# Hand-ordered steps of an attention kernel: subtractions moved from VectorE to GpSimd, one weight operation per step, mask limits called later

## The chip, the cores and the metric

The kernel runs on one core of a Trainium2 chip. The metric is the time of one execution on the device, in microseconds (us). Before the change three runs took 440.40, 440.41 and 440.67 us (median 440.41). The core has five engines that run beside each other: PE (TensorE, matmuls), DVE (VectorE), ACT (ScalarE), POOL (GpSimd) and SP (SyncE, which issues transfers here). PEld is PE's loading of weights.

## The reference

Four batches of 768 tokens with 8 heads of 64 go through an attention with a mask (8 global keys, and the last 96 tokens) and a bias by distance; what comes out goes through a feed-forward stage with a convolution over three tokens and a gate. Everything is in float32, the weights of the second stage come as float64.

```
scores = q @ k.T / sqrt(64) - slope[head] * dist;  scores = where(keep, scores, -1e9)
a = softmax(scores);  x = (a @ v), heads side by side            # 4 x 768 x 512
h = relu(x @ w_in)                                               # 4 x 768 x 1024
conv = cw[0] * h[t-1] + cw[1] * h[t] + cw[2] * h[t+1]
out = (h * sigmoid(conv)) @ w_out                                # 4 x 768 x 512
```

## The kernel before

Attention goes in 32 jobs (a batch, a half `u` of the tokens, a pair of heads) of three blocks of 128 rows. A block is a *step*; there are 96 of them, numbered `s`. In a step PE makes the scores of two heads (L381), DVE adds the bias from a table and takes the row's limit (L408), ACT takes the exponential and its sum (L425), PE transposes the result (L450, L452), ACT copies it out of PSUM (L455), and PE multiplies by v (L501). Because PE's single-pass float32 format (fp32r) is not exact enough by itself, every operand of the feed-forward stage is kept as a high part (rounded to fp32r) and a low part (what the rounding left), and a product is three matmuls: high by high, high by low, low by high.

Steps 0 to 13 (`HAND = 14`) are written out by hand in `by_hand`: there each engine takes its instructions in the order of the code. From step 14 on a scheduler orders the instructions by a model of its own; it may put an instruction that has no one to wait for into an earlier gap. In the first four jobs of the hand-ordered steps the softmax is divided late: PE spreads the inverse sums over a PSUM tile (`spread`, L476), ACT copies it (`factors`, L484), DVE multiplies (`scaled`, L488), ACT rounds the mixed heads to their high part (`mixed_high`, L513) and DVE subtracts to get the low part (`mixed_low`, L517, tile `xl`). In steps 6, 9 and 12 PE takes one slice of the first feed-forward product of a job that is done (`mm1_early`, L560): `wih` by `xh`, `wih` by `xl`, `wil` by `xh`. Some small matmuls on a constant tile (`warm`, L168) stand in every step.

Beside that the weights are turned from float64 words into high and low parts, in 16 pieces of 128x512. For a piece ACT makes a first value from the low words (L305, `weight_tail`), DVE puts in the bits of the high words with two operations (L311, L313), POOL rounds to the high part (L318, `weight_high`), and DVE subtracts for the low part (L324, `weight_low`). `work("dve", 0.1)` takes one operation from a list of these; by hand it is called twice in an even step and once in an odd one. `limits` (L239 to L242) are four tiny DVE operations that test whether the mask's two numbers are in range; only the very end of the program reads what they leave.

Of the kernel before, what the change touches and what calls it, by code (L numbers as in the profile page):

```python
# [9 lines left out]
F32 = mybir.dt.float32  # L10
# [5 lines left out]
ALU = mybir.AluOpType  # L16
# [9 lines left out]
NB = TB // P  # L26
# [14 lines left out]
HAND = 14  # L41
# [26 lines left out]
def fast_path(tc, io):  # L68
    nc = tc.nc
    V, A, G, T = nc.vector, nc.scalar, nc.gpsimd, nc.tensor  # L70
# [95 lines left out]
    def warm(n):  # L166
        for _ in range(n):
            T.matmul(wp[:, TB:], wz, wz, start=True, stop=True)  # L168
# [69 lines left out]
    def limits():  # L238
        V.tensor_scalar(odd[:, 0:1], nl, 1.0, None, ALU.is_lt)  # L239
        V.tensor_scalar(odd[:, 1:2], nl, float(NPREV + 1), None, ALU.is_gt)  # L240
        V.tensor_scalar(odd[:, 2:3], ng, float(NGLOB), None, ALU.is_gt)
        V.tensor_reduce(bad, odd, axis=mybir.AxisListType.X, op=ALU.max)  # L242
        G.memset(ones, 1.0)
# [36 lines left out]
    def weight_planes(i):  # L280
        if i < NK:
            h, l = wih[:, i], wil[:, i]
        else:
            j = i - NK
            h = woh[:, 2 * j : 2 * j + 2].rearrange("p f d -> p (f d)")
            l = wol[:, 2 * j : 2 * j + 2].rearrange("p f d -> p (f d)")
        return (x.rearrange("p (f n) -> p f n", f=NF) for x in (h, l))
# [27 lines left out]
    def weight_high(i, half):  # L315
        t = wt[i, half]
        h, l = weight_planes(i)
        G.tensor_copy(h[:, half * HF : (half + 1) * HF], t)  # L318

    def weight_low(i, half):  # L320
        t = wt[i, half]
        h, l = weight_planes(i)
        sl = slice(half * HF, (half + 1) * HF)
        V.tensor_tensor(l[:, sl], t, h[:, sl].bitcast(F32), ALU.subtract)  # L324

    words, top, TOP = [], {}, 0x38000000

# [33 lines left out]
    st_s, st_pt, pv, xt, sums = {}, {}, {}, {}, {}  # L361
# [4 lines left out]
    def free(s):  # L366
        return s < NB * FREE

    def scores(s):
        m, i = steps[s]  # L370
        b, u, hp = jobs[m]
        w = NKC[u]
        first = u == 0 and i == 0
        n = W0 if first else WIN
        k0 = key_start(u, i)
        both = ps_s.tile([P, 2, 256], F32, tag="s", name=f"s{s}")
        sp = [both[:, 0], both[:, 1]]
        for j in range(2):
            if m < NATIVE:
                rq, rk = raw[m]  # L380
                last_mm[s] = T.matmul(  # L381
                    sp[j][:, :n],
                    rq[:, j, i * P : (i + 1) * P],
                    rk[:, k0 : k0 + n],
                    start=True,
                    stop=True,
                )
                continue
            qh, ql, kk = qk[m]
            for n_, (q_, st, sp_) in enumerate(((qh, True, False), (ql, False, True))):  # L390
                last_mm[s] = T.matmul(  # L391
                    sp[j][:, :n],
                    q_[:, j * TB + i * P : j * TB + (i + 1) * P],
                    kk[:, j * w + k0 : j * w + k0 + n],
                    start=st,
                    stop=sp_,
                )
        st_s[s] = (sp, n, first)
# [73 lines left out]
    def spread(m):  # L472
        for i in range(NB):
            for j in range(2):
                k = 2 * (NB + i) + j
                T.matmul(  # L476
                    wp[64 * j : 64 * j + 64, i * P : (i + 1) * P],
                    sums[m][:, k : k + 1].to_broadcast([P, D]),
                    ident, start=True, stop=True,
                )  # L480
# [31 lines left out]
        xt[m] = (xh, xl)  # L512
        A.activation(xh, pv[m], AF.Copy)  # L513

    def mixed_low(m):
        xh, xl = xt[m]
        cur["mixed"] = V.tensor_tensor(xl, pv[m], xh.bitcast(F32), ALU.subtract)  # L517

    def mixed(m):
        mixed_high(m)  # L520
        mixed_low(m)

    def ends(s):
        return s >= 0 and s % NB == NB - 1
# [189 lines left out]
    queue, cur = [], {}  # L714
# [25 lines left out]
    chores = {"dve": [], "pool": []}  # L740

    def work(eng, budget):
        q = chores[eng]
        while q and budget > 0 and q[0][0] <= cur["s"]:
            _, cost, fn, args = q.pop(0)
            fn(*args)
            budget -= cost
# [15 lines left out]

    def piece_high(i, half):
        weight_high(i, half)
        chores["dve"].insert(2, (0, 0.6, piece_low, (i, half)))

    def piece_low(i, half):
        weight_low(i, half)
        done[i, half] = cur["s"]  # L770

    def need(*pieces):
# [19 lines left out]
    def by_hand(s):  # L792
        m, i = steps[s]
        p, q = s - 1, s - 2
        scores(s)
        if q >= 0 and free(q):
            block(*steps[q])
        if ends(q):
            spread(q // NB)
        mm1_early(s)  # L800
        warm(WARM[s + 1])
        if ends(q):
            factors(q // NB)
        if p >= 0 and free(p):
            transposes(p)
        maxima(s)
        exps(s)
        if ends(s - 3):
            mixed_low((s - 3) // NB)
        if ends(p):  # L810
            inverses(p // NB)
        if ends(q):
            scaled(q // NB)
            mixed_high(q // NB)
        if p >= 0 and not free(p):
            normalise(p)
        if i == 0 and m + 1 < NPAIR:
            table(2 * m + 2, X=G)
            table(2 * m + 3, X=G)
        for _ in range(2 - s % 2 if s else 1):  # L820
            work("dve", 0.1)
        if s == HAND - 1:
            mixed_low(q // NB)
        if s == 5:
            limits()
        if s in (4, 6):
            conv_weights((s - 4) // 2)
        work("pool", 1.3)

    hand = True  # L830
    for s in range(len(steps) + LAG_V + 1):
        cur["s"] = s
        m, i = steps[s] if s < len(steps) else (len(jobs), -1)
        if s < HAND:
            by_hand(s)
        else:
            if hand:
                hand = False
                cur["auto"] = True
                manual.__exit__(None, None, None)  # L840
                queue.extend(ffn(0))
            if s < len(steps):
                scores(s)
                maxima(s)
                exps(s)
            e = s - LAG_V - 1
            if e >= SPU and e % SPU == SPU - 1:
                queue.extend(ffn(e // SPU))
            left = SPU - (e + 1) % SPU + 1
            if e + 1 >= len(steps) - SPU:  # L850
                left += 1
            if e < SPU - 1:
                left += SPU
            k = -(-sum(cost for cost, _, _ in queue) // left)
            if ends(e) and not free(e):
                with tc.high_priority():
                    mixed(e // NB)
            if s <= len(steps):
                normalise(s - 1)
            if s < LAG_V + SPU:  # L860
                mm1_early(s)
            k0 = int(k * SHARE[e % 2])
            fill(k0)
            if ends(s - LAG_V) and not free(s - LAG_V):
                values((s - LAG_V) // NB)
            if s < len(steps) + LAG_T and not free(s - LAG_T):
                transposes(s - LAG_T)
            fill(k - k0)
            if s < len(steps):
                budget = DECODE_LATER[min((s - HAND) // 3, len(DECODE_LATER) - 1)]  # L870
                with tc.issue_after(last_ttr[s].ins):
                    work("dve", budget)
                    work("pool", 1.2)
        if s == len(steps):
            for k in range(3):
                check_load()
        if s == HINT:
            with tc.issue_after(last_exp[s].ins):
                tc.mark_branch_hint_location(
                    "general", "LikelyTaken", [mybir.EngineType.Activation]  # L880
                )
        if s == 0:
            for k in range(len(order)):
                chain(*order[k])
            start_piece(0)
            load_v(0)
            start_piece(1)
            load(2)
            start_piece(2)
            load_v(1)  # L890
            start_piece(3)
            load_conv_weights()
        if i < 2:
            prep(m + 1, i)
        if i == 0:
            if 1 <= m < NATIVE - 2:
                load(m + 2)
        elif i == 1 and m + 2 >= NATIVE:
            load(m + 2)
        if m < FREE and s > NB and i == NB - 1:  # L900
            load_v(m + 1)
        elif m > FREE and i == 0:
            load_v(m)
# [203 lines left out]
```

## Time and profile before

| | |
|---|---|
| median of three runs | 440.41 us |
| the profiled execution | 440.63 us, its span in the trace 438.8 us |
| busy: PE / DVE / ACT / POOL | 427.0 / 345.1 / 285.2 / 225.4 us |
| granted clock of PE | 1.0 of full speed throughout |
| steps 0 to 13 in the trace | from about 7 to 43 us |

Busy time is that of the records of an engine. PE's records overlap each other, since matmuls are pipelined, so what one matmul costs is read from the distance between two starts. A record's line (L324) is that of the kernel before; names of tiles stand as written<-read. In the timeline a bracket at a row's end is the engine's idle time before that instruction and what ended it.

### The profile page before, as it was taken

The numbers are of one execution on the slowest core, as the hardware profiler recorded it, in microseconds if no ns is written. First come the engines' busy times: TensorE is split into PE (matmuls) and PEld (weight loads), VectorE is DVE, ScalarE is ACT, GpSimd is POOL, SyncE is SP. The second block draws the span as 40 slices with busy tenths as digits, with TensorE's granted clock in tenths as the row PEclk, the third lists the DMA queues.
The fourth block names the chain that finished last, engine by engine and source line by source line (L and its number), as shares of the span: only waits on it lengthen the run. The fifth ranks groups of instructions, "written<-read, shape, count | busy, mean of one in ns | idle before, by whom it ended". The sixth has DMA issues, their size and how long they took to land.

```text
span 438.8 us, 10010 instructions
## 1 busy us (share of the span) xinstructions
PE 427.0 (97%) x3566; PEld 404.6 (92%) x3566; DVE 345.1 (79%) x894; ACT 285.2 (65%) x771; POOL 225.4 (51%) x324
## 2 busy tenths in 40 slices
PE   9899979999999999999999999999999999999996
PEld 8677967889999999999999999999999999999996
DVE  6797899979999988767989797867999868556500
ACT  2778688597797866647885767647885866136311
POOL 4312789955735963557668843557668631022000
PEclk9999999999999999999999999999999999999999
DMA  8876864322245234353354224442243467800111
GB/s 256 269 229 183 257 176 154 83 83 91 92 122 160 80 111 136 104 176 94 105 150 152 51 101 134 149 141 85 92 162 120 124 242 240 271 26 0 49 50 55
DMA packets 22570, 58.77 MB, mean 134 GB/s; under 512 B 2928, under 2 KB 6256, under 8 KB 22512
## 3 DMA queue, kind: packets, MB, share of 16 engines
q1 hardware_dynamic: 18608, 51.56, 37.7%
q10 hardware_dynamic: 3904, 6.49, 4.1%
q8 instruction: 30, 0.49, 0.5%
q14 instruction: 28, 0.23, 0.2%
HBM read 51.75 MB, written 6.29 MB: 132 GB/s over the span
## 4 chain that ended last, share of the span: by engine, by line
PE 78%; DVE 12%; ACT 6%; issue 2%; POOL 1%; ACTq 0%; DVEq 0%; POOLq 0%
PE o L652 27%; PE h L539 25%; PE pv L501 7%; PE s L391 5%; PE t L450 4%; PE t L452 3%; DVE s L408 3%; PE s L381 3%; ACT pbuf L425 3%; PE warm L168 2%; DVE c L587 2%; DVE c L586 1%; PE o L922 1%; ACT pt L455 1%; DVE w L313 1%
## 5 line engine op out<-in xcount | busy, mean ns | idle before, releaser
L443 POOL TENSOR_SCALAR pbuf<-pbuf,mm 128x232 f32<-128x232 f32 (+1 forms) x156 | 112.3, 732 | 65.1 <-DVE mm L437 41.0
L425 ACT ACTIVATE pbuf<-s,mm 128x232 f32<-128x232 f32 (+1 forms) x192 | 83.0, 440 | 51.8 <-DVE mm L408 38.1
L408 DVE CUSTOM_DVE_ANT_0 s<-s,tab 128x232 f32<-128x232 f32 (+1 forms) x192 | 73.1, 381 | 9.8 <-PE s L391 4.8
L652 PE MATMUL o<-woh,gh 128*128 128x256 f32 x368 | 77.2, 288 | 0.0
L652 PE MATMUL o<-wol,gh 128*128 128x256 f32 x368 | 76.1, 282 | 0.0
L585 POOL TENSOR_SCALAR c<-hbuf,cw 128x382 f32<-128x382 f32 (+1 forms) x64 | 46.1, 723 | 57.8 <-ACT hbuf L549 55.1
L652 PE MATMUL o<-woh,gl 128*128 128x256 f32 x368 | 72.9, 279 | 0.0
L455 ACT ACTIVATE pt<-t 128x512 f32<-128x512 f32 (+1 forms) x96 | 53.7, 566 | 15.0 <-PE t L452 11.5
L539 PE MATMUL h<-xh,wih 128*128 128x384 f32 x252 | 58.2, 348 | 0.3 <-ACT ob L658 0.2
L539 PE MATMUL h<-xl,wih 128*128 128x384 f32 x252 | 58.0, 345 | 0.0
L652 PEld LDWEIGHTS o<-wol,gh 128*128 128x128 f32 x368 | 57.2, 189 | 0.7
L652 PEld LDWEIGHTS o<-woh,gh 128*128 128x128 f32 x368 | 56.6, 189 | 0.7
L539 PE MATMUL h<-xh,wil 128*128 128x384 f32 x252 | 56.7, 344 | 0.0
L652 PEld LDWEIGHTS o<-woh,gl 128*128 128x128 f32 x368 | 56.2, 189 | 0.1
L586 DVE SCALAR_TENSOR_TENSOR c<-hbuf,cw,c 128x382 f32<-128x382 f32 (+1 forms) x64 | 45.2, 712 | 13.4 <-POOL c L585 13.0
L450 PE MATMUL t<-ident,pbuf 128*128 128x128 f32 x192 | 47.6, 276 | 0.9 <-POOL pbuf L443 0.9
L539 PEld LDWEIGHTS h<-xh,wih 128*128 128x128 f32 x252 | 43.4, 189 | 1.4 <-ACT x L484 0.5
L539 PEld LDWEIGHTS h<-xh,wil 128*128 128x128 f32 x252 | 43.8, 188 | 0.6
L549 ACT ACTIVATE hbuf<-h 128x384 f32<-128x384 f32 x64 | 31.2, 492 | 20.2 <-PE h L539 20.1
L587 DVE SCALAR_TENSOR_TENSOR c<-hbuf,cw,c 128x382 f32<-128x382 f32 (+1 forms) x64 | 43.4, 681 | 0.5
L539 PEld LDWEIGHTS h<-xl,wih 128*128 128x128 f32 x252 | 43.3, 189 | 0.3
L501 PE MATMUL pv<-pt,v 128*64 128x128 f32 (+1 forms) x664 | 40.9, 268 | 0.9 <-ACT pt L455 0.9
(123 smaller groups left out, 844.6 us busy)
## 6 DMA issues: line engine op xcount, KB each, us to landing
v<-in_vv SPq DMA_DIRECT2D x32, 384.0 KB, 3.7
wr<-in_w SPq DMA_DIRECT2D x16, 512.0 KB, 4.4
check<-in_w SPq DMA_DIRECT2D x16, 512.0 KB, 4.1
rq<-in_qk SPq DMA_DIRECT2D x20, 384.0 KB, 3.2
rk<-in_qk SPq DMA_DIRECT2D x12, 504.0 KB, 4.0
out<-ob ACTq DMA_DIRECT2D x23, 256.0 KB, 2.5
rk<-in_qk SPq DMA_DIRECT2D x8, 400.0 KB, 3.6
qz<-in_qt SPq DMA_DIRECT2D x22, 96.0 KB, 4.7
```

Of the source, the lines that this page charges most:

```text
L408: last_ttr[s] = V.tensor_tensor_reduce(out=sp[j][:, :n], in0=sp[j][:, :n], in1=tb, scale=-0.125, scalar=3.0e38, op0=ALU.add, op1=ALU.min, ...
L425: last_exp[s] = A.activation(pb[:, j * WIN : j * WIN + n], sp[j][:, :n], AF.Exp, bias=mm[:, j : j + 1], scale=-1.0, accum_out=total[:, j : ...
L443: G.tensor_scalar(x, x, inv, 1.0, ALU.mult, ALU.mult)
L450: T.transpose(pt[:, 0, j], pb[:, j * WIN : j * WIN + P], ident)
L455: last_ev[s] = A.activation(sb[:, :k], pt[:, :k], AF.Copy)
L501: T.matmul(pv[m][64 * j : 64 * j + 64, i * P + q : (i + 1) * P], vt[m][:n, i, c, 64 * j : 64 * j + 64], sb[:n, c, j, q:], start=c == 0, st ...
L539: T.matmul(ps[:, :TB], w_[:, k, fs], x_, start=part == 0 and k == 0, stop=part == 2 and k == NK - 1,)
L549: A.activation(half, ps[:, :TB], AF.Relu, scale=0.5)
L585: G.tensor_scalar(c, *tap(1), 1.0, ALU.mult, ALU.mult)
L586: V.scalar_tensor_tensor(c, *tap(0), c, ALU.mult, ALU.add)
L587: V.scalar_tensor_tensor(c, *tap(2), c, ALU.mult, ALU.add)
L652: T.matmul(ps[:, c], g_[:, f], w_[:, f, c], start=f == part == k == 0, stop=f == NF - 1 and part == 2 and k == 1,)
```

## The change

Low parts of weights whose rounding falls in a hand-ordered step are made by POOL, right behind that rounding, and so are the low parts of the mixed heads of jobs 0 to 2; `work("dve", 0.1)` is called once in each hand-ordered step; `limits` is called after the last step.

```diff
--- before.py
+++ after.py
@@ -317,11 +317,11 @@
         h, l = weight_planes(i)
         G.tensor_copy(h[:, half * HF : (half + 1) * HF], t)
 
-    def weight_low(i, half):
+    def weight_low(i, half, X):
         t = wt[i, half]
         h, l = weight_planes(i)
         sl = slice(half * HF, (half + 1) * HF)
-        V.tensor_tensor(l[:, sl], t, h[:, sl].bitcast(F32), ALU.subtract)
+        X.tensor_tensor(l[:, sl], t, h[:, sl].bitcast(F32), ALU.subtract)
 
     words, top, TOP = [], {}, 0x38000000
 
@@ -512,9 +512,9 @@
         xt[m] = (xh, xl)
         A.activation(xh, pv[m], AF.Copy)
 
-    def mixed_low(m):
+    def mixed_low(m, X=V):
         xh, xl = xt[m]
-        cur["mixed"] = V.tensor_tensor(xl, pv[m], xh.bitcast(F32), ALU.subtract)
+        cur["mixed"] = X.tensor_tensor(xl, pv[m], xh.bitcast(F32), ALU.subtract)
 
     def mixed(m):
         mixed_high(m)
@@ -763,10 +763,13 @@
 
     def piece_high(i, half):
         weight_high(i, half)
-        chores["dve"].insert(2, (0, 0.6, piece_low, (i, half)))
-
-    def piece_low(i, half):
-        weight_low(i, half)
+        if cur["s"] < HAND:
+            piece_low(i, half, G)
+        else:
+            chores["dve"].insert(2, (0, 0.6, piece_low, (i, half, V)))
+
+    def piece_low(i, half, X):
+        weight_low(i, half, X)
         done[i, half] = cur["s"]
 
     def need(*pieces):
@@ -806,7 +809,7 @@
         maxima(s)
         exps(s)
         if ends(s - 3):
-            mixed_low((s - 3) // NB)
+            mixed_low((s - 3) // NB, G)
         if ends(p):
             inverses(p // NB)
         if ends(q):
@@ -817,12 +820,9 @@
         if i == 0 and m + 1 < NPAIR:
             table(2 * m + 2, X=G)
             table(2 * m + 3, X=G)
-        for _ in range(2 - s % 2 if s else 1):
-            work("dve", 0.1)
+        work("dve", 0.1)
         if s == HAND - 1:
             mixed_low(q // NB)
-        if s == 5:
-            limits()
         if s in (4, 6):
             conv_weights((s - 4) // 2)
         work("pool", 1.3)
@@ -872,6 +872,7 @@
                     work("dve", budget)
                     work("pool", 1.2)
         if s == len(steps):
+            limits()
             for k in range(3):
                 check_load()
         if s == HINT:
```

The order in which each engine then has its instructions differs most in these places. Numbers behind a name tell buffers apart and are counted anew in each program. On POOL, from the first rounding of a weight piece (step 2) on, first before, up to step 11:

```order
L318 CAST wih<-w_0_279 128x512
L221 TENSOR_SCALAR tab<-setup 128x360 x2
L318 CAST wih<-w_0_282 128x512
L243 MEMSET misc 128x1
L221 TENSOR_SCALAR tab<-setup 128x360 x2
L318 CAST wih<-w_0_316 128x512
L318 CAST wih<-w_0_397 128x512
L318 CAST wih<-w_1_474 128x512
L318 CAST wih<-w_1_548 128x512
```

and after, up to step 8 (`wil` is the low part of a piece, `xl` that of the mixed heads):

```order
L318 CAST wih<-w_0_279 128x512
L324 TENSOR_TENSOR wil<-w_0_279,wih 128x512
L221 TENSOR_SCALAR tab<-setup 128x360 x2
L318 CAST wih<-w_0_282 128x512
L324 TENSOR_TENSOR wil<-w_0_282,wih 128x512
L517 TENSOR_TENSOR xl_391<-x_377,xh_390 128x384
L221 TENSOR_SCALAR tab<-setup 128x360 x2
L318 CAST wih<-w_0_350 128x512
L324 TENSOR_TENSOR wil<-w_0_350,wih 128x512
L517 TENSOR_TENSOR xl_509<-x_495,xh_508 128x384
L318 CAST wih<-w_0_427 128x512
L324 TENSOR_TENSOR wil<-w_0_427,wih 128x512
```

Each rounding now has a subtraction behind it, and the first `xl` stands behind the second piece's rounding and subtraction. On DVE, the weight operations and the mixed heads of steps 4 and 5 before:

```order
L488 TENSOR_TENSOR x_380<-pv_287,x_380 128x384
L311 SCALAR_TENSOR_TENSOR w_0_316<-wr_0_247,w_0_316 128x512
L324 TENSOR_TENSOR wil<-w_0_279,wih 128x512
L250 TENSOR_SCALAR setup<-setup 128x24
L252 TENSOR_SCALAR cw<-setup 128x24
L253 SCALAR_TENSOR_TENSOR cw<-setup,cw 128x24
L408 ISA s_404,mm_422<-s_404,tab 128x232
```

and after:

```order
L488 TENSOR_TENSOR x_377<-pv_287,x_377 128x384
L313 SCALAR_TENSOR_TENSOR w_0_282<-wr_0_247,w_0_282 128x512
L250 TENSOR_SCALAR setup<-setup 128x24
L252 TENSOR_SCALAR cw<-setup 128x24
L253 SCALAR_TENSOR_TENSOR cw<-setup,cw 128x24
L408 ISA s_402,mm_420<-s_402,tab 128x232
```

What stands in step 4 is now the second bit operation of piece 1, which its rounding on POOL needs; before, that operation stood in step 3. On ACT, the end of step 12 and step 13 before:

```order
L425 ACTIVATE pbuf_215,mm_684<-s_661,mm_684 128x232 x2
L431 ACTIVATE mm_684<-mm_684,misc 128x2
L305 ACTIVATE w_1_693<-wr_1_519 128x512
L305 ACTIVATE w_0_761<-wr_0_625 128x512
L484 ACTIVATE x_719<-warm 128x384
L425 ACTIVATE pbuf_216,mm_721<-s_700,mm_721 128x232 x2
```

and after:

```order
L425 ACTIVATE pbuf_215,mm_676<-s_653,mm_676 128x232 x2
L431 ACTIVATE mm_676<-mm_676,misc 128x2
L484 ACTIVATE x_712<-warm 128x384
L425 ACTIVATE pbuf_216,mm_714<-s_693,mm_714 128x232 x2
L431 ACTIVATE mm_714<-mm_714,misc 128x2
L513 ACTIVATE xh_721<-x_712 128x384
L441 ACTIVATE pbuf_215<-pbuf_215,mm_676 128x232
L305 ACTIVATE w_1_728<-wr_1_540 128x512
L305 ACTIVATE w_0_756<-wr_0_620 128x512
```

Two first values of weight pieces (L305) that stood ahead of the last `factors` now stand behind it. And on DVE, ahead of step 0, where `limits` (L239 to L242) stand after:

```order
L209 SCALAR_TENSOR_TENSOR loc<-setup,num,ge 128x128
L239 TENSOR_SCALAR misc<-num 128x1
L240 TENSOR_SCALAR misc<-num 128x1
L241 TENSOR_SCALAR misc<-num 128x1
L210 SCALAR_TENSOR_TENSOR setup<-setup,num,loc 128x128
L242 TENSOR_REDUCE misc<-misc 128x1
L213 SCALAR_TENSOR_TENSOR loc<-keep,num,loc 128x8
```

Before, these four stood in step 5; the scheduler has put them among the first operations on the mask.

## Rows read from the trace of the kernel before

**Rows 1.** windows of all engines: start:end, length, busy us (instructions), PE clock, DMA.

```profile
20.00:40.00 20.00, 18.95 (x186) 14.94 (x186) 17.99 (x65) 14.55 (x48) 3.25 (x4) 1.00 0.67 198
...
60.00:80.00 20.00, 17.21 (x128) 14.55 (x128) 18.77 (x56) 14.20 (x43) 17.51 (x27) 1.00 0.51 159
...
200.00:300.00 100.00, 100.00 (x851) 97.07 (x850) 83.49 (x220) 68.37 (x184) 63.59 (x82) 1.00 0.38 117
```

**Rows 2.** PE in order of time: start, length, instruction, [idle before <- what ended it].

```profile
21.39 0.62 PE L501 MATMUL spare<-pt,v 128*64 128x128 f32 x8 [0.68 <-ACT pt L455]
...
22.22 0.34 PE L560 MATMUL h<-xl,wih 128*128 128x384 f32 x1
...
29.85 0.33 PE L560 MATMUL h<-xl,wih 128*128 128x384 f32 x1
...
37.70 0.34 PE L560 MATMUL h<-xl,wih 128*128 128x384 f32 x1
...
41.31 1.00 PE L381 MATMUL s<-rk,qz 128*128 128x232 f32 x4
```

**Rows 3.** DVE by line and shape: busy us, mean ns | idle before.

```profile
L324 DVE TENSOR_TENSOR wil<-w,wih 128x512 fp32r<-128x512 f32 x8 | 5.4, 678 | 0.0
...
L517 DVE TENSOR_TENSOR xl<-x,xh 128x384 fp32r<-128x384 f32 x4 | 2.2, 554 | 0.0
```

**Rows 4.** POOL in order of time.

```profile
8.01 0.68 POOL L217 TENSOR_TENSOR setup<-setup,keep 128x232 f32<-128x232 f32 x1
...
9.57 0.10 POOL L235 MEMSET misc<- 128x1 f32 x1
...
24.50 1.00 POOL L318 CAST wih<-w 128x512 fp32r<-128x512 f32 x1 [5.84 <-DVE w L313]
27.83 0.62 POOL L318 CAST wih<-w 128x512 fp32r<-128x512 f32 x1 [2.32 <-DVE w L313]
```

**Rows 5.** DVE in order of time, where it stands beside POOL.

```profile
20.52 0.18 DVE L253 SCALAR_TENSOR_TENSOR cw<-setup,cw 128x24 f32<-128x24 uint32 x1
...
24.96 0.59 DVE L255 SCALAR_TENSOR_TENSOR setup<-setup 128x24 int32<-128x24 int32 x1
```

**Rows 6.** DVE in order of time, steps 4 and 5.

```profile
19.03 0.68 DVE L311 SCALAR_TENSOR_TENSOR w<-wr,w 128x512 int32<-128x512 int32 x1
...
20.62 0.40 DVE L408 CUSTOM_DVE_ANT_0 s<-s,tab 128x232 f32<-128x232 f32 x1
```

**Rows 7.** ACT in order of time, job 1.

```profile
27.60 0.54 ACT L513 ACTIVATE xh<-x 128x384 fp32r<-128x384 f32 x1
```

**Rows 8.** DVE in order of time, steps 10 and 11.

```profile
34.70 0.68 DVE L313 SCALAR_TENSOR_TENSOR w<-wr,w 128x512 int32<-128x512 int32 x1
...
35.90 0.40 DVE L408 CUSTOM_DVE_ANT_0 s<-s,tab 128x232 f32<-128x232 f32 x1
...
36.72 0.55 DVE L517 TENSOR_TENSOR xl<-x,xh 128x384 fp32r<-128x384 f32 x1
```

**Rows 9.** ACT in order of time, steps 12 and 13.

```profile
40.81 1.21 ACT L305 ACTIVATE w<-wr 128x512 f32<-128x512 uint32 x2
41.93 0.47 ACT L484 ACTIVATE x<-warm 128x384 f32<-128x384 f32 x1
```

**Rows 10.** DVE in order of time, ahead of step 0.

```profile
7.22 0.23 DVE L215 TENSOR_SCALAR loc<-keep,num 128x8 f32<-128x8 f32 x1
7.86 0.30 DVE L408 CUSTOM_DVE_ANT_0 s<-s,tab 128x128 f32<-128x128 f32 x1 [0.41 <-PE s L381]
```

**Rows 11.** DVE in order of time, limits in step 5.

```profile
22.51 0.15 DVE L239 TENSOR_SCALAR misc<-num 128x1 f32<-128x1 f32 x1
...
22.88 0.29 DVE L408 CUSTOM_DVE_ANT_0 s<-s,tab 128x128 f32<-128x128 f32 x1
```

**Rows 12.** POOL by line and shape: busy us, mean ns | idle before.

```profile
L443 POOL TENSOR_SCALAR pbuf<-pbuf,mm 128x232 f32<-128x232 f32 x134 | 100.5, 761 | 47.6 <-DVE mm L437 27.4 <-ACT pbuf L425 8.4 <-ACT pt L455 4.3
...
L216 POOL TENSOR_SCALAR keep<-loc 128x232 f32<-128x232 f32 x1 | 0.4, 387 | 5.3 <-DVE loc L215 5.3
```

## The prediction

> **What bounds the kernel now.** I read the windows first. PE stands in nearly every microsecond: 18.95 of 20 us in the window of the hand-ordered steps, all 100 of the window from 200 to 300 us, and only 17.21 from 60 to 80 us [rows 1]. DVE, which the change relieves, is at 17.99 of 20 us in the first of these windows, so it looks like the bottleneck by its share, but its share doesn't say that PE waits for it. That is read from PE's own timeline: in steps 5 to 7 its one long wait is 0.68 us at 21.39, and what ends it is ACT's copy (L455), not DVE [rows 2]. Around it matmuls follow each other without a gap, `warm` ones among them. So the hand-ordered steps are bound by PE, with about 1 us of waiting in 20, and a shorter DVE can give back no more than a part of that. What counts is whether something PE waits for gets later. The three early slices of the feed-forward product are such places: PE takes `xl` at 22.22, 29.85 and 37.70 us [rows 2], in its fixed order, and everything behind it in that order waits too.
>
> **What DVE loses.** In the hand-ordered steps six subtractions for weights at 0.68 us and three for mixed heads at 0.55 us leave DVE [rows 3]: 6 x 0.68 + 3 x 0.55 = 5.7 us of records. The number of bit operations doesn't change (13 calls in place of 19, and the six subtractions are gone), so the same seven pieces are begun and six finished when step 14 comes. I cost this gain at nothing of itself, since PE hides it: PE's next instruction doesn't come earlier when the bias (L408) is done earlier. Transfers of weight words are issued when L313 has read a buffer, so half of them now go one step later; they are used several steps on, and I cost that at nothing too.
>
> **What POOL gets.** Nowhere before does POOL subtract a tile of this size. The nearest row is its addition of two SBUF tiles, 128x232 in 0.68 us (L217); its smallest instruction, a memset, is 0.10 us [rows 4]. Taking 0.10 as fixed: 0.10 + 0.58 x 512/232 = 1.37 us for a weight piece and 0.10 + 0.58 x 384/232 = 1.05 us for mixed heads. I take these, since the row has the same operation with two inputs. The lower end is POOL's rounding, one input, 0.62 us for 512 columns [rows 4], so 0.47 for 384. The upper end is the pace of L443, whose mean is 761 ns where a like operation by itself took 387 ns [rows 12]: a factor of 1.97, thus 2.7 and 2.07 us.
>
> The rounding itself took 0.62 us at 27.83 and 1.00 us at 24.50 [rows 4]. At 24.96 a DVE operation on 24 columns took 0.59 us, where its like took 0.18 us [rows 5]: it ends when POOL's rounding ends. POOL and DVE thus hold each other up where DVE reads two SBUF tiles. The Trainium skill says the same as a rule (SBUF — State Buffer, section "Who interferes with whom"): a DVE instruction with two SBUF inputs and a GpSimd instruction that reads SBUF exclude each other, and the later one blocks until the first is through; these two rows agree. So on POOL a chain of rounding, subtraction, `xl` isn't only slower than on DVE, a DVE bit operation can come in between.
>
> **Step 6.** DVE's bit operation at 19.03 in step 4 is now piece 1's second one (L313) in place of L311 [rows 6]. It starts no earlier, because the multiplication ahead of it hangs on ACT and PE. Two such operations fill 34.70 to 35.90 [rows 8], so one is 0.60 us: done at 19.63. POOL rounds until 20.25 and subtracts until 21.62. DVE's next bias operation comes at 20.02 in place of 20.62 [rows 6], as L324 is gone, takes some 0.97 us, and the bit operation behind it is then blocked from 20.99 to 21.62. If POOL goes on at once, `xl` is done at 21.62 + 1.05 = 22.67; if DVE's 0.60 us come first, at 23.27. PE wanted it at 22.22. It is late by 0.45 to 1.05 us; I take 0.75.
>
> **Step 9.** The high part of job 1 ends at 27.60 + 0.54 = 28.14 [rows 7], POOL has long done its piece, and `xl` would be there at 28.14 + 1.05 = 29.19, ahead of 29.85 [rows 2]. No new wait; both move by the same 0.75.
>
> **Step 12.** L313 for piece 4 starts at 34.70 [rows 8], now 35.45, and ends at 36.05. Rounding to 36.67, subtraction to 38.04, `xl` to 39.09, or 39.69 behind a DVE bit operation. PE wanted it at 37.70: 1.39 to 1.99 late in all, I take 1.7. Before, DVE made this `xl` at 36.72 [rows 8], right behind its bias operation, because there it had no piece ahead of it.
>
> **Step 13.** Here something is won. PE is done with what `factors` (L484) reads when it begins the next scores at 41.31 [rows 2], but ACT is at two first values of weight pieces from 40.81 on and comes to L484 at 41.93 [rows 9]. They now stand behind. That gives 41.93 - 41.31, less a hand-over, 0.5 us; L484 is followed by the exponentials that step 15's scores wait for, so the 0.5 us is on the path.
>
> **The limits.** They aren't at the end: in the order they stand ahead of step 0. Their cost there is what it was in step 5, 22.88 - 22.51 = 0.37 us [rows 11]. Before step 0 DVE has 0.41 us of idle time [rows 10], which hides it on DVE; POOL's part of the table, which waits for L215, gets later by 0.37 and step 1's first bias operation by some 0.1. In step 5 the removal is hidden by PE like the rest.
>
> **The sum.** 1.7 - 0.5 + 0.1 = +1.3 us at step 14. From there on PE's order is nearly that of before and PE is full, so I carry it to the end. Against the profiled execution of 440.63 us (438.8 of span and 1.83 around it) that is 441.93; the median lies 0.22 lower, so 441.7 us.
>
> The Trainium skill (GPSIMD Engine Reference, section "Elementwise — side-by-side cycle accounting") gives 2.6 cycles per element for two inputs because both share one read port, at 1.2 GHz: an estimate of 1.11 and 0.83 us and a fixed part. With 0.1 us fixed, step 6 would be late by 0.5, step 12 by 1.1 in all, and the sum +0.7, 441.1 us. Its table under "Engine selection" says of an elementwise operation on a tile to use VectorE; the row of L217 bears that out.
>
> **The rivals.**
> - *POOL keeps up, faster (0.25).* If the subtraction runs at the pace of the rounding, `xl` is there at 20.25 + 0.62 + 0.47 = 21.34, before PE wants it, and in step 12 too. Then the change has only gains: of the 0.68 us wait for ACT at most all (ACT's L305 no longer stands ahead of that copy), and 0.5 in step 13, less 0.1: -1.1 us, 439.3. For it: POOL is almost idle in these steps, 3.25 of 20 us [rows 1]. Against it: L217. The point from which it decides is where rounding, subtraction and `xl` together take under 2.6 us (22.22 - 19.63); by my values they take 3.04.
> - *The delay is taken up later, no change (0.2).* From 60 to 80 us PE stands still for 2.8 us [rows 1], waiting for others. If the scheduler's other order there has fewer such waits, the 1.3 us vanish: 440.4. Against it: what PE waits for there hangs on steps that begin later too.
> - *The two engines block each other at L443's pace (0.1).* With 2.7 and 2.07 us, step 6 is late by 2.8 to 3.4 and step 12 by 6.1 to 6.7; +5.9, 446.1. Against it: that mean is of later stages, where DVE's convolution and gate operations stand beside POOL.
> - My forecast has 0.45; its own range is 441.2 to 443.2.
>
> **How the numbers follow.** A difference under 0.2% (0.9 us) can't be told from none, thus faster is below 439.5 and slower above 441.3. The forecast lies above it; with the skill's figure it would lie just within. Slower: 0.45 and 0.1, that is 0.55. Same: 0.2. Faster: 0.25. The range reaches from the faster rival, 439.3, to 444.0, where half of the rival with blocking engines is left out.
>
> **What would show it.** Right: POOL's subtractions of 128x512 at 1.2 to 1.5 us; waits of PE of about 1 us for `xl` from POOL in steps 6 and 12, none in step 9; DVE's bit operations of odd steps stretched beyond 0.68 us; L484 of step 13 right behind PE; PE's later timeline moved by 1 to 2 us. Wrong: no wait of PE on L517; subtractions near 0.7 us; or the same step 14, and a difference that arises only between 50 and 140 us.

## The result and the profile after: 2.2 us slower

The changed kernel takes 442.65 us (median of six runs, 442.39 to 444.34), the one before in the same runs 440.49; the ratio is 1.0057, with a 95% interval of [1.0046, 1.0068]. Three slow runs are not counted in this document (469.48 and 1465.27 us of the kernel before, 469.55 us of e3 below). The changed kernel is slower, as forecast, and by more than the 1.3 us forecast. The profiled execution took 443.03 us with a span of 441.1, against 440.63 and 438.8: +2.3 us in the span. The busy time of PE is 427.0 us in both, so PE has no more work; it stands idle more. Where, the windows tell first.

The windows after, in the columns of [rows 1]:

```profile
20.00:40.00 20.00, 16.82 (x164) 12.86 (x162) 16.21 (x51) 13.43 (x44) 12.37 (x13) 1.00 0.63 203
60.00:80.00 20.00, 17.33 (x139) 14.15 (x135) 18.95 (x55) 16.37 (x49) 19.18 (x26) 1.00 0.53 166
200.00:300.00 100.00, 100.00 (x850) 97.10 (x849) 82.75 (x216) 68.40 (x187) 62.97 (x81) 1.00 0.38 118
```

From 20 to 40 us PE was busy 18.95 us and is now 16.82; from 60 to 80 it gains 0.1. The loss is in the hand-ordered steps and nowhere else in these three. Between 12 and 44 us PE's waits of the changed kernel, grouped (us in total, times, longest), have a first line that the kernel before doesn't have:

```profile
PE h L560 <- POOL xl L517: 2.5, 2, 1.3
```

PE of the changed kernel in order of time, at the places of [rows 2]:

```profile
20.82 0.62 PE L501 MATMUL spare<-pt,v 128*64 128x128 f32 x8 [0.30 <-ACT pt L455]
21.37 0.45 PE L560 MATMUL h<-xh,wih 128*128 128x384 f32 x1
23.00 0.44 PE L560 MATMUL h<-xl,wih 128*128 128x384 f32 x1 [1.19 <-POOL xl L517]
...
30.12 0.62 PE L501 MATMUL pv<-pt,v 128*64 128x128 f32 x8 [0.46 <-ACT pt L455]
...
30.95 0.34 PE L560 MATMUL h<-xl,wih 128*128 128x384 f32 x1
...
40.09 0.44 PE L560 MATMUL h<-xl,wih 128*128 128x384 f32 x1 [1.32 <-POOL xl L517]
...
43.80 1.00 PE L381 MATMUL s<-rk,qz 128*128 128x232 f32 x4
...
45.48 0.85 PE L381 MATMUL s<-rk,qz 128*128 128x232 f32 x3
```

And the scores of step 15 in the kernel before:

```profile
43.33 1.05 PE L381 MATMUL s<-rk,qz 128*128 128x232 f32 x4
```

A wait isn't a delay. In step 6 PE stands 1.19 us for `xl`, but the matmul is only 23.00 - 22.22 = 0.78 us later than before, because PE's matmuls ahead of it start 0.57 us earlier (20.82 against 21.39). Of this, 0.38 us is the wait for ACT's copy, which shrank from 0.68 to 0.30 us. The other 0.19 is there before: step 6's scores start at 19.91 against 20.10. That much says little, since over all eleven profiles of this document these scores start between 19.78 and 20.10 us. The delay against before then goes +0.78 (step 6), +1.10 (step 9), +2.39 (step 12), +2.49 (step 14's scores, 43.80 against 41.31) and +2.15 (step 15's scores, 45.48 against 43.33). The last matmul starts at 437.22 against 434.92, +2.30: what is lost by step 15 is carried to the end.

What PE waits for is on POOL. POOL of the changed kernel in order of time, to set beside [rows 4]:

```profile
19.58 0.61 POOL L318 CAST wih<-w 128x512 fp32r<-128x512 f32 x1 [2.07 <-DVE w L313]
20.28 1.27 POOL L324 TENSOR_TENSOR wil<-w,wih 128x512 fp32r<-128x512 f32 x1
21.51 1.44 POOL L517 TENSOR_TENSOR xl<-x,xh 128x384 fp32r<-128x384 f32 x1
...
29.10 1.00 POOL L517 TENSOR_TENSOR xl<-x,xh 128x384 fp32r<-128x384 f32 x1 [2.60 <-ACT xh L513]
...
31.40 1.30 POOL L324 TENSOR_TENSOR wil<-w,wih 128x512 fp32r<-128x512 f32 x1
36.57 0.61 POOL L318 CAST wih<-w 128x512 fp32r<-128x512 f32 x1 [3.87 <-DVE w L313]
37.26 1.82 POOL L324 TENSOR_TENSOR wil<-w,wih 128x512 fp32r<-128x512 f32 x1
39.03 1.00 POOL L517 TENSOR_TENSOR xl<-x,xh 128x384 fp32r<-128x384 f32 x1
```

Two chains stand there without idle time: rounding, subtraction, `xl`. They begin at 19.58 and 36.57 and end when PE's wait ends. In step 9 `xl` finds POOL free. Where no DVE operation holds it up, a subtraction takes 1.27 to 1.30 us and an `xl` 1.00. The 1.44 and the 1.82 stand beside bit operations of DVE, and some of these are stretched too. DVE of the changed kernel in order of time:

```profile
20.97 1.13 DVE L311 SCALAR_TENSOR_TENSOR w<-wr,w 128x512 int32<-128x512 int32 x1
...
31.58 1.67 DVE L311 SCALAR_TENSOR_TENSOR w<-wr,w 128x512 int32<-128x512 int32 x1
...
35.82 0.68 DVE L313 SCALAR_TENSOR_TENSOR w<-wr,w 128x512 int32<-128x512 int32 x1
...
37.24 0.69 DVE L311 SCALAR_TENSOR_TENSOR w<-wr,w 128x512 int32<-128x512 int32 x1
```

The one at 31.58 began when POOL's subtraction of 31.40 to 32.70 was under way, and ends 0.55 us behind it. The one at 37.24 began 0.02 us before POOL's subtraction and took its ordinary 0.69, while POOL's took 1.82 instead of 1.28. In these two pairs, whoever comes first keeps the other out.

ACT of the changed kernel in order of time; the last row is to be set beside the second of [rows 9]:

```profile
28.90 0.68 ACT L305 ACTIVATE w<-wr 128x512 f32<-128x512 uint32 x1
29.46 0.61 ACT L455 ACTIVATE pt<-t 128x512 f32<-128x512 f32 x1
...
44.06 0.49 ACT L484 ACTIVATE x<-warm 128x384 f32<-128x384 f32 x1 [0.67 <-PE warm L168]
```

L484 now follows 44.06 - 43.80 = 0.26 us behind the start of the scores, before 41.93 - 41.31 = 0.62: the gain of step 13 is 0.36 us. The first two rows concern step 9; there L455 stood ahead of L305 in the kernel before:

```profile
28.36 0.60 ACT L455 ACTIVATE pt<-t 128x512 f32<-128x512 f32 x1 [0.23 <-PE t L452]
```

### The profile page after: what moved, and what is told of

Same layout as the page of the kernel before. It is cut to its first block, busy times and chain, and to the rows that moved or that the text cites. A ratio compares the mean times of both kernels' runs of the same rounds, so it can differ in the third digit from the quotient of the medians.

```text
span 441.1 us, 10009 instructions
## 1 busy us (share of the span) xinstructions
PE 427.0 (97%) x3566; PEld 403.6 (91%) x3566; DVE 342.8 (78%) x885; ACT 285.2 (65%) x771; POOL 240.1 (54%) x333
## 4 chain that ended last, share of the span: by engine, by line
PE 78%; DVE 9%; ACT 5%; POOL 5%; issue 2%; DMA 1%; ACTq 0%; DVEq 0%
PE o L652 29%; PE h L539 25%; PE pv L501 7%; PE s L391 6%; PE t L450 4%; PE t L452 3%; ACT pbuf L425 2%; POOL pbuf L443 2%; DVE s L408 2%; DVE c L587 1%; PE s L381 1%; DVE c L586 1%; PE o L923 1%; DMA nn<-in_nn 1%; POOL wil L324 1%
## 5 line engine op out<-in xcount | busy, mean ns | idle before, releaser
L443 POOL TENSOR_SCALAR pbuf<-pbuf,mm 128x232 f32<-128x232 f32 (+1 forms) x156 | 114.4, 744 | 68.7 <-DVE mm L437 50.5
L585 POOL TENSOR_SCALAR c<-hbuf,cw 128x382 f32<-128x382 f32 (+1 forms) x64 | 47.7, 747 | 57.5 <-ACT hbuf L549 54.5
L455 ACT ACTIVATE pt<-t 128x512 f32<-128x512 f32 (+1 forms) x96 | 54.1, 566 | 21.3 <-PE t L452 17.6
L450 PE MATMUL t<-ident,pbuf 128*128 128x128 f32 x192 | 48.4, 277 | 2.8 <-POOL pbuf L443 2.0
L452 PE MATMUL t<-ident,pbuf 128*128 128x128 f32 x160 | 39.9, 276 | 2.5 <-POOL pbuf L443 2.1
```

Of the source, the lines that this page charges most:

```text
L443: G.tensor_scalar(x, x, inv, 1.0, ALU.mult, ALU.mult)
L450: T.transpose(pt[:, 0, j], pb[:, j * WIN : j * WIN + P], ident)
L452: T.transpose(pt[:, 1, j], pb[:, j * WIN + P : j * WIN + 256], ident)
L455: last_ev[s] = A.activation(sb[:, :k], pt[:, :k], AF.Copy)
L585: G.tensor_scalar(c, *tap(1), 1.0, ALU.mult, ALU.mult)
```

## The experiments

The theory: the loss is `xl` on POOL, late because the weight piece's subtraction stands ahead of it there. The rivals: the stretched DVE operations make the loss; the weight pieces on POOL by themselves make it; the place of the limits makes it. Edits are to the changed kernel where nothing else is said, and "ratio" is the time over that of the kernel before.

**Mixed low parts back on DVE (e1).** Weights stay on POOL.

```diff
-            mixed_low((s - 3) // NB, G)
+            mixed_low((s - 3) // NB)
```

> The changed kernel with the low parts of the mixed heads (xl) back on DVE; the low parts of the weights stay on POOL. Theory (PE waits for xl, which stands on POOL behind a rounding and a subtraction): PE's waits of 1.19 and 1.32 us go, 440.0 to 440.8 us. Rival (DVE's bit operations, stretched to 1.1 to 1.7 us by POOL's subtractions, are what delays the steps): they stay stretched, 442 us or more.

Measured: 439.95 us (11 runs, 439.81 to 440.61); against before the ratio is 0.999 [0.9981, 0.9998]. PE's waits for POOL are gone, as the theory has it, and the time lies 0.05 us below its range. The part of the change that is left is a gain, small but just clear of 1, and this version beats both kernels. PE of this version in order of time:

```profile
22.02 0.44 PE L560 MATMUL h<-xl,wih 128*128 128x384 f32 x1 [0.20 <-DVE xl L517]
...
37.62 0.33 PE L560 MATMUL h<-xl,wih 128*128 128x384 f32 x1
...
41.22 1.00 PE L381 MATMUL s<-rk,qz 128*128 128x232 f32 x4
...
42.83 1.05 PE L381 MATMUL s<-rk,qz 128*128 128x232 f32 x4
```

Its DVE in order of time:

```profile
20.96 1.00 DVE L517 TENSOR_TENSOR xl<-x,xh 128x384 fp32r<-128x384 f32 x1
21.89 0.96 DVE L311 SCALAR_TENSOR_TENSOR w<-wr,w 128x512 int32<-128x512 int32 x1
...
30.49 1.67 DVE L311 SCALAR_TENSOR_TENSOR w<-wr,w 128x512 int32<-128x512 int32 x1
...
36.25 0.55 DVE L517 TENSOR_TENSOR xl<-x,xh 128x384 fp32r<-128x384 f32 x1
```

DVE is blocked as before (1.67 us, and its own `xl` at 1.00 instead of 0.55), and nobody waits for it long. So the rival with the stretched DVE operations falls, and the one with the weight pieces by themselves. Step 15's scores come 45.48 - 42.83 = 2.65 us earlier than in the changed kernel; that is the price of `xl` on POOL. Against before they come 0.50 us earlier: step 14's scores 0.09, and the rest is the gain of step 13. At the end of the span (438.6 against 438.8) 0.2 us of this are left.

**Weights' low parts back on DVE (e2).** The counterpart: only `xl` on POOL, and weight operations called twice in even steps as before.

```diff
-        if cur["s"] < HAND:
-            piece_low(i, half, G)
-        else:
-            chores["dve"].insert(2, (0, 0.6, piece_low, (i, half, V)))
+        chores["dve"].insert(2, (0, 0.6, piece_low, (i, half, V)))
...
-        work("dve", 0.1)
+        for _ in range(2 - s % 2 if s else 1):
+            work("dve", 0.1)
```

> The changed kernel with the low parts of the weights back on DVE and two weight operations in even steps; only xl is on POOL. Theory (POOL's queue ahead of xl is what makes it late): xl takes 1.0 us right behind the high part and is there before PE wants it, 440.2 to 440.9 us. Rival (any subtraction on POOL for PE is too slow by itself, 1.0 us in place of DVE's 0.5): PE waits about 0.5 us in steps 6, 9 and 12, 441.5 to 442 us.

Measured: 441.14 us (440.92 to 441.99), ratio 1.0017 [1.0008, 1.0026]. No wait of PE for `xl` is left, as the theory says, but the time isn't that of before. It lies between the two ranges, since another wait came. It begins on DVE, here in order of time:

```profile
20.16 0.97 DVE L250 TENSOR_SCALAR setup<-setup 128x24 int32<-128x24 int32 x1
```

POOL at the same time:

```profile
20.09 1.01 POOL L517 TENSOR_TENSOR xl<-x,xh 128x384 fp32r<-128x384 f32 x1 [2.65 <-ACT xh L513]
```

ACT, which waits for DVE:

```profile
21.23 0.32 ACT L251 ACTIVATE setup<-setup,misc 128x24 int32<-128x24 int32 x1 [0.65 <-DVE cw L252]
21.45 0.58 ACT L455 ACTIVATE pt<-t 128x512 f32<-128x512 f32 x1
```

And PE, which waits for ACT:

```profile
22.08 0.62 PE L501 MATMUL spare<-pt,v 128*64 128x128 f32 x8 [1.44 <-ACT pt L455]
22.63 0.45 PE L560 MATMUL h<-xh,wih 128*128 128x384 f32 x1
22.91 0.34 PE L560 MATMUL h<-xl,wih 128*128 128x384 f32 x1
```

An operation of DVE on 24 columns (L250, the convolution's weights), 0.17 us in the kernel before, stands beside POOL's `xl` and takes 0.97; ACT's L251 waits for the one behind it (L252); the copy that PE waits for (L455) stands behind L251. The `xl` matmul is 22.91 - 22.22 = 0.69 us late. Here, then, a blocked DVE operation does cost, by the two engines behind it.

**The same with the convolution's weights a step later (e6).** To e2 is added:

```diff
-        if s in (4, 6):
-            conv_weights((s - 4) // 2)
+        if s in (5, 7):
+            conv_weights((s - 5) // 2)
```

> e2 (only xl on POOL) with the two halves of the decoding of the convolution's weights in steps 5 and 7 in place of 4 and 6. Theory (e2's loss of 0.7 us is DVE's tiny L250, which took 0.97 us in place of 0.17 beside POOL's xl, and ACT's L251 that waits for it): 440.2 to 440.6 us. Rival (xl on POOL delays PE in another way): 441.0 to 441.3 us as e2.

Measured: 440.29 us (440.06 to 441.45), ratio 1.0002 [0.9993, 1.001], in the theory's range: the loss of e2 is gone, and with it the doubt about its cause. In this run `xl` on POOL, with no weight subtraction ahead of it and without L250 beside it, costs nothing that can be measured.

**`xl` ahead of the weight subtraction (e5).** All the work of the change stays on POOL; only the order there is another.

```diff
-            piece_low(i, half, G)
+            chores["pool"].insert(0, (cur["s"] + 1, 0.6, piece_low, (i, half, G)))
```

> The changed kernel with the weights' subtraction on POOL taken one step later, so that xl stands on POOL right behind the rounding. Both subtractions stay on POOL. Theory (what stands ahead of xl on POOL is the loss): PE no longer waits for xl, step 13's gain stays, 439.9 to 440.6 us. Rival (an xl on POOL costs its 1.0 us wherever it stands, by holding up DVE as in e2): 440.9 to 441.5 us.

Measured: 440.14 us (440.01 to 440.77), ratio 0.9997 [0.9988, 1.0005], in the theory's range. Its POOL in order of time:

```profile
19.76 0.61 POOL L318 CAST wih<-w 128x512 fp32r<-128x512 f32 x1 [2.18 <-DVE w L313]
20.33 1.00 POOL L517 TENSOR_TENSOR xl<-x,xh 128x384 fp32r<-128x384 f32 x1
21.29 1.75 POOL L324 TENSOR_TENSOR wil<-w,wih 128x512 fp32r<-128x512 f32 x1
```

PE's `xl` matmul, without a wait:

```profile
21.83 0.34 PE L560 MATMUL h<-xl,wih 128*128 128x384 f32 x1
```

The same operations on the same engine; `xl` is ready at 21.33, PE doesn't wait here or in step 12, and 2.5 us are back. This is the run that decides: the weight subtraction ahead of `xl` on POOL is the loss, not POOL's pace by itself. Step 15's scores start at 42.62, 0.71 us earlier than before, but the last transfer is issued only 0.19 us earlier (435.45 against 435.64): of what is gained in these steps, little reaches the end.

**The slice one step later (e3).** PE asks for `xl` a step later; POOL and DVE are as in the changed kernel.

```diff
-        if k < NK - 1 and s >= 6 + NB * k and done.get((k, 0), s) < s - 1:
+        if k < NK - 1 and s >= 7 + NB * k and done.get((k, 0), s) < s - 1:
```

> The changed kernel with each early slice of the feed-forward product one step later (steps 7, 10, 13), so that xl has some 2 us more. Theory (the wait for xl is the loss): no wait of PE on POOL, 440.0 to 441.0 us, though all of POOL's and DVE's work is as in the changed kernel. Rival (DVE's stretched bit operations or ACT's moved first values are the loss): 442.2 to 442.8 us.

Measured: 440.97 us (ten runs, 440.19 to 441.26), ratio 1.001 [1.0001, 1.0019], in the theory's range. No wait for POOL is left, so the rivals fall, the stretched DVE operations and ACT's moved first values. What is left, 0.3 us by step 15 (43.64 against 43.33), has a new wait in it: the third slice's matmuls now stand in step 13 ahead of the `warm` matmuls, for which `factors` (L484) waits. PE of this version:

```profile
42.77 0.79 PE L539 MATMUL h<-xh,wih 128*128 128x384 f32 x3 [0.64 <-ACT x L484]
43.64 1.05 PE L381 MATMUL s<-rk,qz 128*128 128x232 f32 x4
```

**The limits back in step 5 (e4).**

```diff
+        if s == 5:
+            limits()
...
-            limits()
```

> The changed kernel with the limits called in step 5 again. If their place ahead of step 0 costs 0.1 us or nothing, as the prediction has it: 442.3 to 442.7 us, no difference to the changed kernel that can be told. Rival (they delay the first tables by the full 0.37 us and more): 442.0 or less.

Measured: 444.01 us (442.48 to 444.83, six runs), ratio 1.0073 [1.0055, 1.009]: both ranges missed, this one is slower than the changed kernel. In its profile step 6's scores start 0.11 us earlier (19.80 against 19.91). The other two pairs of profiles that differ ahead of this point by the limits' place alone give 0.13 (e8 against e1) and 0.01 us (e10 against e11), so the limits ahead of step 0 cost some 0.1 us or less. What comes then is something else. Its windows of one microsecond, the clock third from the end:

```profile
22.00:23.00 1.00, 0.09 (x1) 0.09 (x1) 0.82 (x7) 0.62 (x2) 0.93 (x3) 0.94 1.01 408
23.00:24.00 1.00, 1.00 (x5) 0.69 (x6) 0.97 (x5) 0.00 (x0) 0.92 (x2) 0.50 0.39 154
...
25.00:26.00 1.00, 1.00 (x5) 0.90 (x4) 0.27 (x1) 0.47 (x1) 0.92 (x2) 0.50 0.48 86
26.00:27.00 1.00, 1.00 (x10) 0.70 (x9) 0.26 (x1) 0.83 (x5) 0.59 (x1) 0.85 0.80 324
```

PE's row that ends the wait:

```profile
22.91 0.69 PE L560 MATMUL h<-xl,wih 128*128 128x384 f32 x1 [1.21 <-POOL xl L517]
```

After a wait of 1.21 us the granted clock is 0.50 (1.2 GHz) for more than 3 us, and the matmul takes 0.69 us instead of 0.44; step 14's scores start 45.26 - 43.80 = 1.46 us later than in the changed kernel. There the like wait, 1.19 us, left the clock at 1.00. The single runs agree: the four that list a mean clock of 0.996, as this profile does, took 443.99 to 444.83 us, and the two at 1.0 and 0.999 took 442.48 and 443.07 us, which is like the changed kernel's runs. (The mean alone doesn't say where the clock fell: one run of e3 lists 0.996 too and isn't longer, 440.90 us.) So by these runs it is the fall of the clock, and not the limits' place by itself, that separates this version from the changed kernel; why the clock fell here is open. Of the changed kernel's own runs only the one of 444.34 us lists 0.996; it has no profile of its own, so that the same happened there isn't shown.

**Limits in step 5 with `xl` on DVE (e8).** e1 and e4 together.

> e1 (xl on DVE, weights' low parts on POOL) with the limits called in step 5 again. If the place of the limits is worth 0.1 us or nothing: 439.8 to 440.1 us. Rival (their place ahead of step 0 costs 0.4 us): 439.5 to 439.6 us.

Measured: 440.14 us (439.79 to 440.73), ratio 0.9994 [0.9985, 1.0002]. That is 0.04 us above the first range and far from the rival's. It can't be told from e1: the limits' place is worth nothing that can be measured in the time.

**Matmuls on a constant in the place of the wait (e10, e11).** 20 more `warm` matmuls ahead of the slice's second matmul in steps 6 and 12; e11 to the changed kernel, e10 to e4.

```diff
+        hand_ = cur["s"] in (6, 12)
...
+            if part == 1 and hand_:
+                warm(20)
```

> e4 (changed kernel, limits in step 5) with 20 more of the warm matmuls (1.2 us of PE) ahead of the slice's second matmul in steps 6 and 12, where PE stood and waited for xl. If e4's loss beyond the changed kernel (444.0 against 442.65 us) is the fall of PE's clock behind that wait, and not the place of the limits: 442.3 to 442.8 us, with no run near 444. If it is the limits: 444 again.

> The changed kernel with the same 20 more warm matmuls ahead of the slice's second matmul in steps 6 and 12. The wait for xl itself stays, so it stays slow: 442.3 to 442.8 us; the single runs near 444 (as 444.34 of the changed kernel) go if they are the fall of the clock. Rival (the wait isn't what counts, or the matmuls are added to it): 443.5 to 445 us.

Measured: 444.02 us, ratio 1.0083 [1.007, 1.0096], for e10, and 443.75 us, ratio 1.0076 [1.0064, 1.0088], for e11. Both miss the first range and lie where the rival had them; but neither rival's reason is what the profiles show. PE of e11, where L563 is the L560 of the others:

```profile
21.59 1.29 PE L168 MATMUL warm<-setup 128*128 128x128 bf16 x20
...
40.04 0.45 PE L563 MATMUL h<-xl,wih 128*128 128x384 f32 x1 [0.19 <-POOL xl L517]
```

1.29 us of extra matmuls in each of two steps leave the `xl` matmul where it was (40.04 against 40.09), so PE really had nothing to do there, and the matmuls are not added to the wait. In both profiles the steps ran at a clock of 1.00, and the last transfer is issued at 437.54 (e10) and 437.87 us (e11), not later than the 437.94 of the changed kernel. But the spans are 442.1 and 442.4: 4.5 us lie behind that issue, where it is 3.2 in the changed kernel and in all the others. No engine is busy in these 1.3 us. It is the last store itself that ends later. The time from issue to landing of the two stores of `oc` (shortest, median, longest), in the changed kernel:

```profile
DMA to landing us min/median/max: 1.7/1.7/1.7
```

and in e10:

```profile
DMA to landing us min/median/max: 2.2/2.6/3.0
```

In e11 it is 2.2 and 3.1. The packets of the trace show where: of the last store's 128 packets of 1 KB, 120 have begun by 438.9 us in e10, and the other 8 begin one after another from 439.35 to 440.07. Just ahead of these 8 ends a packet of 16 KB (438.00 to 439.37) on queue q8, which the profile lists under "instruction". In e11 it is the same, 8 packets from 439.70 on behind one that ends at 439.71. In the nine other profiles the last such packet is through before the store's first packet begins. So the 1.3 us fit a loading of instructions that falls into the last store, at a place that 40 more matmuls have moved; no run tests this. Without them e10 and e11 would stand at some 442.7 and 442.4 us (an estimate: the medians less the 1.3 us of the two profiles), where they were expected. That supports the fall of the clock as e4's loss, and doesn't prove it.

## Why the prediction was right, and where it was small

- *What bounds the kernel.* Right. DVE is busy 342.8 us instead of 345.1, and that gives nothing by itself; what counted was a tile that PE takes in a fixed order.
- *What DVE loses, at nothing.* Right within 0.2: in e1 and e8, where PE hardly waits for `xl`, step 14's scores are 0.09 and 0.20 us earlier than before. (The calls are 14 in place of 20, not 13 and 19; the difference of six stands.)
- *POOL's durations.* 1.27 to 1.30 us measured for 1.37, 1.00 for 1.05 (worked out exactly, the prediction's sums give 1.38 and 1.06): the row of L217 was a good base and its fixed part was taken too low. Between 384 and 512 columns lie 0.27 to 0.28 us for 128 columns, that is 2.1 to 2.2 ns each; that pace with some 0.17 us fixed gives L217's 0.68 us for 232 columns too. The 2.6 cycles at 1.2 GHz that the Trainium skill gives (GPSIMD Engine Reference, section "Elementwise — side-by-side cycle accounting") are 2.17 ns, so these rows agree with it. The estimate made from it came out too low all the same, 0.7 instead of 2.3: like the forecast, it had only half of one DVE operation in each chain, and nothing of step 9's wait.
- *Step 6.* 0.78 measured for 0.75. The bit operation that was feared between POOL's operations (20.97, 1.13 us) did come, and made `xl` 1.44 us. The 0.75 was the mean of two orders, and for the one that came the prediction had 1.05; that the mean fits so well is in part luck.
- *Step 9.* No wait for `xl`, as forecast, but the carry was 1.10, not 0.75. Of the 0.32 us more than in step 6, 0.1 is step 6's `xl` matmul, which holds PE 0.28 us behind the wait and 0.18 without one, and the rest is a wait: that for ACT's copy grew from 0.24 to 0.46 us, since L305 (28.90) now stands ahead of L455, which before came first. The prediction had moved the weight operations on DVE and POOL and not followed ACT's first values, which the same list sets free.
- *Step 12, the mis-sized term.* 2.39 measured for 1.7. From its lower end (1.39): L313 began 0.37 later than assumed (35.82 for 35.45; step 9's excess), from L313's start to the subtraction's start it took 37.26 - 35.82 = 1.44 for the 1.22 assumed, 0.22 more, and the subtraction held POOL 0.40 longer (1.77 to the next start, for 1.37), as DVE's bit operation had come 0.02 us ahead of it. That is 1.39 + 0.37 + 0.22 + 0.40, and 0.01 of small differences. Of this only half of one DVE operation in between, 0.3, was in the 1.7.
- *Step 13.* 0.36 measured for 0.5: L484 starts 0.26 us behind the scores, where a hand-over of some 0.1 had been taken off.
- *The limits.* 0.1 us or less, as forecast, but not by the forecast's way: on DVE they cost 0.05 us and not 0.37 (from L209's start to L213's it is 5.22 - 4.39 = 0.83 us with them and 5.11 - 4.33 = 0.78 before). No run could tell it in the total.
- *The sum.* 2.39, +0.10 to step 14 (again the matmul behind the wait), -0.34 to step 15, +0.15 by the end: +2.3, for 1.7 - 0.5 + 0.1 = 1.3. The last term isn't explained; in the other profiles the difference to the kernel before changes from step 15 to the end by -0.2 (e2, e4) to +0.5 us (e5). The errors of the terms nearly all have one sign, but the measured 442.65 us stays within the forecast's own range, 441.2 to 443.2.
- *The signs.* All came but the last: PE's later timeline moved by 2.2 to 2.3 us and not by 1 to 2.
- *The rivals.* POOL doesn't keep up: 1.27 and 1.00 us, not the pace of the rounding; yet in another order on POOL (e5) PE doesn't wait for `xl` at all, so the rival failed by the order as much as by the pace. Nothing is taken up later. The engines do block each other, and POOL's two chains were held up by 0.44 and 0.54 us, far from L443's factor of 1.97 throughout. (That rival's sum is 6.4 - 0.5 + 0.1 = 6.0, thus 446.4 us and not 446.1.)

## What to carry to other kernels

When work moves to an idle engine, look at the one tile there that the bounding engine takes in a fixed order, and put it ahead of the work that nobody waits for: that order alone was worth 2.5 us here, and the pace of the engine nothing that could be measured. Where two engines hold each other up, as DVE and POOL do here, whoever comes second pays, so list both sides' instructions in that stretch and the waits behind each, the tiny ones too. A list that feeds several engines moves all of them: follow each engine's first operation for a piece, not only those that the diff names.

## What the runs showed of the hardware

- A DVE operation with one input of 24 columns (L250) took 0.97 us beside POOL's subtraction of 1.01, and 0.17 in the kernel before. The Trainium skill (SBUF — State Buffer, section "Who interferes with whom") says that a `tensor_scalar` can contend with GpSimd when its operands allow a mode that uses two ports. These rows agree, and show that a tiny one can be held for nearly the whole of the other engine's instruction.
- Two like waits of PE, 1.19 and 1.21 us in the same place, left the granted clock at 1.00 in one profile and at 0.50 for 3.4 us in the other.
- With 40 more matmuls, none of them near the end, the time from the last store's issue to the end of the span grew from 3.2 to 4.5 us. The store's last 8 packets of 1 KB stand behind a packet of 16 KB of an instruction queue; that it holds them up is argued from their order in time, in e10 and e11, and not tested.
